# Moving the scatters of slot numbers and the first expert's weights in an attention + mixture-of-experts kernel

## The chip, the core and the metric

The kernel runs on one core of a Trainium2 chip. The core has a matrix engine (PE, with its weight loads shown apart as PEld), a vector engine (DVE), a scalar engine (ACT), a general engine (POOL), and a queue engine (SP) that mostly issues DMAs; POOL issues DMAs too, the indexed ones among them. Each engine runs its own instructions in order and waits on semaphores for the others. SBUF is the on-chip memory of 128 partitions, PSUM holds what PE writes, DRAM is outside. The metric is the time of one execution in microseconds (us): before the change the median of 3 runs is 855.22 us (852.43 to 856.94).

## The reference

Two stages. Attention with a mask by hash: 6 sign bits of each query and key (against `proj`) give a bucket, and only pairs in one bucket are scored. Then a mixture of experts, where each of the 3072 tokens goes to the one expert with the largest gate logit.

```python
q_bits = (np.einsum('bhsd,dk->bhsk', q, proj) > 0)            # the same for k; 4 batches, 8 heads, 768 tokens, width 64
mask = q_bucket[:, :, :, None] == k_bucket[:, :, None, :]
scores = np.where(mask, scale * q @ k^T, -1e9)
attn = softmax(scores) @ v                                     # tokens x 512 = x
expert_idx = argmax(x @ w_gate)                                # 8 experts
gate_w = softmax(x @ w_gate) at expert_idx
y[token] = gate_w * relu(x @ w1[e]) @ w2[e]                    # w1 512x1024, w2 1024x512, e = expert_idx
```

## The kernel before, in words

**Attention** is cut into 16 groups g (a pair of heads of one batch; 4 groups a batch) and each group into 6 *cycles* c (so c runs from 0 to 97, with a tail of two; r = c % 6 is the place in the group). In a cycle PE does, in this order: two pv steps of an older unit (L337), the gate-and-output product `tok` (L353) of one older still, 12 transposes of probabilities (L305), and two units of scores for the newest (L269 and L271: the rows of bucket bits and low parts, then the high part). DVE takes the row maximum of each unit (L276 to L278), and ahead of that, in the same cycle, scales `tok`'s product (L366) and copies one of three transposed tiles (L325). ACT takes the exponentials (L286) and copies the other two. A cycle's program is also each engine's order: nothing is reordered, the schedule is written by hand.

**The heads of the next group** are prepared on POOL while a group runs. Each of the two heads is split into a rounded part and a remainder, in 12 steps by the table `SPLITS`, two in each of the six cycles: (0,0) and (0,1) in r = 0, (0,2) and (0,3) in r = 1, then the same for head 1 in r = 2 and 3, (0,4) and (0,5) in r = 4, (1,4) and (1,5) in r = 5. The last four are a copy of 64 partitions (L179) and a subtraction on the upper 64 (L180). In r = 1 POOL also turns the hash products into bits (L232, L234); SP stores them to DRAM (`masks`, L245) and POOL reads them back into the heads' tiles in r = 3 (L249, a DMA on POOL's queue). The stores of results and the loads of the next heads stand behind L245 on SP.

**Routing.** When the tokens of half a batch are through (b, hf), the generator `route` computes their expert and their slot in that expert's list, some DVE operations at a time: `go(q, 2)` in each cycle runs the next two pieces between the transposed copies and the row maxima. Its last piece, before the change, is three indexed DMAs on POOL (L437), each of which scatters 128 slot numbers into the DRAM table `slot_token`. Each has a small memset (L436) before it. `go` stands ahead of the split steps of its cycle, so on POOL the scatters come first in that cycle. For batches 0 and 1 they fall in c = 35 and 59 (first half, r = 5) and c = 42 and 66 (second half, r = 0), for batch 2 in c = 83 (r = 5) and c = 86 (r = 2, after POOL's part of c = 85). Batch 3's follow after the last cycle.

**The first expert** (the fullest after batch 2, `pick_first` in c = 85) is started while attention still runs. Its weights come in 8 loads of 512 KB (`raw`, two buffers, L587 on SP) and are taken apart in 16 parts, `chunk_part`: a rounded copy (L597) and the remainder (L598), both on POOL for this expert. Each second part frees a buffer and issues the next load. Before the change 12 of the 16 parts run in c = 86 to 95, one or two a cycle, and four in c = 96 and 97. In c = 90, SP reads the first 256 slots (`gather_ix`, L614) and POOL gathers their rows (`gather_rows`, L622). `xt` transposes those in c = 94 to 97, and `mm1(0, 0)` is the first product of the experts.

**The experts** follow from about 506 us: for each of nine phases, products with w1 (L657) and w2 (L683, L700), while POOL, ACT and DVE take the next weights apart (L600, L601) and POOL gathers and scatters rows (L622, L711).

## Time and profile before

| what | us |
|---|---|
| median of the runs (lowest, highest) | 855.22 (852.43, 856.94) |
| profiled execution, its own time | 851.78 |
| its span, first to last instruction | 850.0 |
| PE busy in the span | 796.8 (94%) |
| DVE, ACT, POOL busy | 530.9, 439.4, 492.1 |
| mean granted clock of PE | 0.974 |

A profile row gives an instruction's start, its duration, engine, line, what it writes and reads, and in brackets how long the engine sat idle before it and what ended that. "x2" merges neighbours. A row of the view of waits gives who waited for whom, the total, how often and the longest. A row of the view of stretches gives the stretch, its length, each engine's busy time and number of instructions, then the granted share of PE's clock, the share of time in which the DMA engines were busy, and GB/s. For PE, busy time near the whole span means that what matters is where it stood idle, and where its clock was cut.

### The profile page before, as it was taken

How to read it: one execution, taken by the hardware profiler on the slowest of the kernel's cores; microseconds unless marked ns; L12 is line 12 of the kernel's file. 1: busy time of each engine (PE TensorE's matmuls, PEld its weight loads, DVE VectorE, ACT ScalarE, POOL GpSimd, SP SyncE). 2: the span in 40 equal slices, each digit the busy share in tenths (PEclk: the TensorE clock that was granted, in tenths of full speed). 3: DMA queues.
4: the chain of work that ended last, by engine and by line, in shares of the span. 5: the costliest groups of instructions: out<-in, count | busy, mean ns of one | idle time of the engine just before them, and what ended most of it. 6: DMA issues, size and time to landing. Idle time of an engine off the chain costs nothing. (4 is left out here: it accounts for less than half of the span.)

```text
span 850.0 us, 14119 instructions
## 1 busy us (share of the span) xinstructions
PE 796.8 (94%) x4814; PEld 627.7 (74%) x4814; DVE 530.9 (62%) x1234; ACT 439.4 (52%) x877; POOL 492.1 (58%) x641
## 2 busy tenths in 40 slices
PE   8999999979999969999978898999999999999992
PEld 3677767657777747777645666888999999989782
DVE  6877777858778848778956565454475644434410
ACT  4776767647676746767646461343434343434210
POOL 5876657647856747765665783564363745546401
PEclk9999999989999989999989799999999999999997
DMA  9674587467568739664737251466353635466101
GB/s 232 167 144 82 121 149 149 111 78 129 119 103 154 133 35 138 138 99 93 107 81 112 77 101 20 151 198 189 100 173 106 188 128 165 140 176 181 37 11 32
DMA packets 75804, 103.01 MB, mean 121 GB/s; under 512 B 43972, under 2 KB 48068, under 8 KB 75730
## 3 DMA queue, kind: packets, MB, share of 16 engines
q1 hardware_dynamic: 62610, 86.47, 46.0%
q0 software_dynamic: 13120, 15.61, 7.8%
q8 instruction: 39, 0.64, 0.3%
q14 instruction: 35, 0.29, 0.1%
HBM read 86.65 MB, written 16.35 MB: 121 GB/s over the span
## 5 line engine op out<-in xcount | busy, mean ns | idle before, releaser
L286 ACT ACTIVATE e<-s,m 128x768 f32<-128x768 f32 x192 | 190.4, 992 | 139.9 <-DVE m L278 134.4
L276 DVE TENSOR_REDUCE m<-s 128x1 f32<-128x768 f32 x192 | 182.9, 952 | 84.0 <-PE s L271 79.3
L337 PE MATMUL o<-pt,vt 128*64 128x384 f32 x768 | 150.3, 514 | 0.0
L305 PE MATMUL t<-ident,e 128*128 128x128 f32 x1152 | 144.4, 275 | 1.7 <-ACT pt L327 1.1
L305 PEld LDWEIGHTS t<-ident,e 128*128 128x128 f32 x1152 | 130.7, 142 | 6.8 <-issue 1.8
L657 PE MATMUL t<-xh,w 128*128 128x456 f32 (+6 forms) x672 | 127.2, 346 | 1.2 <-DVE hh L662 1.2
L657 PEld LDWEIGHTS t<-xh,w 128*128 128x128 f32 x672 | 119.1, 188 | 4.5 <-DVE hh L662 1.6
L601 POOL TENSOR_TENSOR w<-raw,w 128x512 fp32r<-128x512 f32 x56 | 72.6, 1305 | 68.5 <-ACT w L600 68.1
L327 ACT ACTIVATE pt<-t 128x512 f32<-128x512 f32 (+1 forms) x194 | 103.8, 592 | 3.1 <-PE t L305 2.4
L601 DVE TENSOR_TENSOR w<-raw,w 128x512 fp32r<-128x512 f32 x56 | 61.0, 1093 | 51.8 <-ACT w L600 43.8
L337 PEld LDWEIGHTS o<-pt,vt 128*64 128x64 f32 x768 | 47.7, 139 | 60.7 <-issue 59.7
L683 PE MATMUL t<-hh,w 128*128 128x456 f32 (+3 forms) x384 | 78.7, 358 | 0.0
L711 POOL DMA_INDIRECT out_dram<-y,ix x27 | 35.2, 1305 | 70.8 <-DVE y L709 61.9
L661 ACT ACTIVATE hh<-t 128x256 fp32r<-128x256 f32 (+7 forms) x64 | 31.3, 490 | 79.6 <-PE t L657 77.3
L683 PEld LDWEIGHTS t<-hh,w 128*128 128x128 f32 x384 | 69.9, 188 | 2.4
L271 PE MATMUL s<-qk 128*128 128x384 f32 x204 | 56.0, 357 | 16.1 <-POOL qk L180 16.1
L325 DVE COPY pt<-t 128x512 f32<-128x512 f32 (+1 forms) x97 | 66.4, 685 | 6.8 <-PE t L305 2.7
L353 PEld LDWEIGHTS t<-gm,ot 128*128 128x128 f32 x192 | 28.6, 189 | 56.7 <-issue 29.5
L662 DVE SCALAR_TENSOR_TENSOR hh<-t,hh 128x256 fp32r<-128x256 f32 (+7 forms) x64 | 35.4, 554 | 51.7 <-ACT hh L661 48.3
L269 PE MATMUL s<-qk 80*128 80x384 f32 x204 | 59.8, 373 | 8.1 <-DMA qk<-masks 4.9
L600 ACT ACTIVATE w<-raw 128x512 fp32r<-128x512 f32 x112 | 66.3, 623 | 0.0
L700 PE MATMUL s<-w,hh 128*128 128x512 f32 (+2 forms) x264 | 66.0, 405 | 0.0
(197 smaller groups left out, 1191.3 us busy)
## 6 DMA issues: line engine op xcount, KB each, us to landing
raw<-in_w_dram SPq DMA_DIRECT2D x64, 512.0 KB
xd<-in_qk_dram SPq DMA_DIRECT2D x36, 384.0 KB
xhe<-in_qk_dram SPq DMA_DIRECT2D x15, 768.0 KB
w<-in_qk_dram SPq DMA_DIRECT2D x28, 384.0 KB
vt<-in_v_dram SPq DMA_DIRECT2D x16, 384.0 KB
x_rows<-xs SPq DMA_DIRECT2D x64, 96.0 KB
masks<-bits SPq DMA_DIRECT2D x15, 192.0 KB
w<-masks POOLq DMA_DIRECT2D x15, 96.0 KB
```

The lines of the kernel that those rows point to most:

```text
L269: nc.tensor.matmul(p[:, a, :HALF], k[0:80, 2, c], k[0:80, 3, a * HALF:(a + 1) * HALF], start=True, stop=False)
L276: nc.vector.tensor_reduce(m[:, 0:1], p[:, :, :HALF], axis=AX.XY, op=OP.max)
L286: nc.scalar.activation(e, p[:, :, :HALF], AF.Exp, bias=m[:, 2:3], scale=m[:, 1:2], accum_out=SM[g, hf][:, t, s:s + 1])
L305: nc.tensor.transpose(p[:, x * 128:(x + 1) * 128], e[w][:, kt // 3, (kt % 3) * 128:(kt % 3) * 128 + 128], ident)
L325: nc.vector.tensor_copy(o, x)
L327: nc.scalar.activation(o, x, AF.Copy)
L337: nc.tensor.matmul(p[s * 64:(s + 1) * 64, :HALF], VT[g][:, kt, s, :], PT[u][:, s, kt, :], start=(kt == 0), stop=(kt == NT - 1))
L600: nc.scalar.activation(w[:, 0, a], r, AF.Copy)
L601: (nc.vector if a % 2 else nc.gpsimd).tensor_tensor(w[:, 1, a], r, w[:, 0, a], op=OP.subtract)
L657: nc.tensor.matmul(p[:, :c], w[:, a, d, fs], x[:, b, d, :c], start=(k == 0), stop=(k == 11))
L683: nc.tensor.matmul(p[:, :c], w[:, a, f % 4, ms], h[b][:, f, :c], start=(k == 0), stop=(k == 23))
L700: nc.tensor.matmul(p[:pw], HH[n][b][:, f, j * pw:(j + 1) * pw], w[:, a, f % 4], start=(k == 0), stop=(k == 23))
```

## The change

Three things move.

1. The scatters leave `route` and become `scatter(b, hf)`. It is called at the end of a cycle's program, after the split steps and the small copies of that cycle. For batches 0 and 1 the calls are in c = 37 and 61 (first half) and c = 43 and 67 (second half), for batch 2 in c = 79 and 85. All of these have r = 1 (the second cycle of a group, which is a pair of heads). Batch 2's first half is routed with four pieces a cycle, so that it is ready in c = 79. After attention, batch 3's scatters stand where they stood.
2. The 16 parts of the first expert's weights run two a cycle in c = 90 to 97. Of each two, the copy of the second goes to DVE; remainders stay on POOL. `raw_load(0, 0)` and `(0, 1)` stay in c = 85.
3. `gather_ix(0)` stays in c = 90, `gather_rows(0)` goes to c = 91.

```diff
-    scat = []
+    scat, SL = [], {}
...
         nc.sync.dma_start(xr[t0 * 128:(t0 + 3) * 128, DM:RW].rearrange("(t p) o -> p t o", p=128), f[:, 3, :, None])
-        yield
+        SL[b, hf] = slot
+
+    def scatter(b, hf):
+        slot = SL.pop((b, hf))
+        t0 = b * NT + hf * 3
         for t in range(3):
             nc.gpsimd.memset(C["spacer"], 0.0)
             st = nc.gpsimd.indirect_dma_start(
...
         if c < 4:
-            nc.gpsimd.tensor_copy(w[:, 0, a], r)
+            (nc.vector if a % 2 else nc.gpsimd).tensor_copy(w[:, 0, a], r)
             nc.gpsimd.tensor_tensor(w[:, 1, a], r, w[:, 0, a], op=OP.subtract)
...
-        for q in routes:
-            go(q, 2)
+        for q, n in routes:
+            go(q, n)
...
         if c >= 24 and c < NC:
             b, q = divmod(c - 24, 24)
+            late = b == B - 2
             if q == 4:
-                routes.append(route(b, 0))
-            if q == (7 if b == B - 2 else 11):
-                routes.append(route(b, 1))
+                routes.append((route(b, 0), 4 if late else 2))
+            if q == (7 if late else 11):
+                routes.append((route(b, 1), 2))
+            if q == (7 if late else 13):
+                scatter(b, 0)
+            if q == (13 if late else 19):
+                scatter(b, 1)
...
-        if NC - 10 <= c < NC:
-            weights(2 if c % 5 == 1 else 1)
...
         if c == NC - 6:
             gather_ix(0)
+        if c == NC - 5:
             gather_rows(0)
-        if c >= NC:
+        if c >= NC - 6:
             weights(2)
...
     go(last[0], 9)
+    scatter(B - 1, 0)
...
     go(last[1], 9)
+    scatter(B - 1, 1)
```

How the rows move on the engines. First POOL around the scatters of batch 0's first half. Before, in c = 35 (qk and xd are the heads' tile and the loaded head, slot_token the table, DMASW are the semaphores of POOL's own DMAs):

```order
L373 COPY lg<-xs 128x16 [waits DVE_49,Pool_49]
L436 MEMSET spacer 1x1
L437 DMA slot_token<-tokid_i,slot 25600x1
L436 MEMSET spacer 1x1 [waits Pool_49]
L437 DMA slot_token<-tokid_i,slot 25600x1
L436 MEMSET spacer 1x1 [waits Pool_49]
L437 DMA slot_token<-tokid_i,slot 25600x1
L179 CAST qk<-xd 64x384
L180 TENSOR_TENSOR qk<-xd,qk 64x384 [waits DMASW6_49,DMASW5_49,DMASW4_49]
```

The L180 that follows (head 1's first remainder, step (1,4)) waits for the three scatters themselves. In the changed kernel, from the third scatter of c = 37 on (w_2259 and w_2394 are the two heads' tiles of the next group):

```order
L441 DMA slot_token<-tokid_i,slot 25600x1
L173 CAST w_2394<-w_69 128x768 [waits DMAHW3_49,DMAHW4_49,DMASW1_49,PE_49]
L175 CAST w_2394<-w_69 128x768
L373 COPY lg<-xs 128x16 [waits DVE_49]
L177 TENSOR_TENSOR w_2394<-w_69,w_2394 80x384 [waits Pool_49]
L177 TENSOR_TENSOR w_2394<-w_69,w_2394 80x384
L249 DMA w_2259<-masks 16x4x384 [waits DMAHW4_49,DMASW7_49]
L249 DMA w_2394<-masks 16x4x384 [waits Pool_49]
L373 COPY lg<-xs 128x16 [waits DVE_49]
L179 CAST w_2259<-w_69 64x384
L180 TENSOR_TENSOR w_2259<-w_69,w_2259 64x384 [waits DMASW5_49,DMASW6_49,DMASW4_49,Pool_49]
```

The wait for the scatters now stands on step (0,4) of r = 4, with the splits of r = 2 and 3 and both mask reads between. The mask reads are now behind three scatters on POOL's own queue.

Second, POOL in c = 86 and 87. Before (w_5373 is the first weight chunk, w_5369 the last group's second head):

```order
L175 CAST w_5369<-xd 128x768
L373 COPY lg<-xs 128x16 [waits DVE_49]
L597 CAST w_5373<-raw 128x512 [waits DMAHW2_49,PE_49]
L598 TENSOR_TENSOR w_5373<-raw,w_5373 128x512 [waits Pool_49]
L597 CAST w_5373<-raw 128x512
L598 TENSOR_TENSOR w_5373<-raw,w_5373 128x512 [waits Pool_49]
L177 TENSOR_TENSOR w_5369<-xd,w_5369 80x384 x2
L249 DMA qk<-masks 16x4x384 [waits DMAHW7_49,DMASW6_49]
```

Now:

```order
L175 CAST w_5369<-xd 128x768
L373 COPY lg<-xs 128x16 [waits DVE_49]
L177 TENSOR_TENSOR w_5369<-xd,w_5369 80x384 [waits Pool_49]
L177 TENSOR_TENSOR w_5369<-xd,w_5369 80x384
L249 DMA qk<-masks 16x4x384 [waits DMAHW7_49]
```

Nothing that waits for a weight load stands ahead of the last group's splits and masks.

Third, DVE between c = 91 and 92 in the changed kernel (w_5597 is the first weight chunk there):

```order
L276 TENSOR_REDUCE m<-s 128x1 [waits PE_49,Activation_49]
L277 TENSOR_SCALAR m<-m 128x1 [waits DVE_49]
L278 TENSOR_SCALAR m<-m 128x1 [waits DVE_49]
L601 CAST w_5597<-raw 128x512 [waits DMAHW3_49]
L366 TENSOR_TENSOR xs<-t,r 128x144 [waits DMAHW5_49,DMAHW6_49,PE_49,Pool_49]
L325 COPY pt<-t 128x2x2x128 [waits PE_49]
```

Before, L366 follows L278 directly there. The new cast waits for a weight load's landing, and L366 and L325, which free the PSUM tiles that PE writes next, are behind it.

## The prediction

> **What bounds the kernel now.** I began with the page: PE is busy for 796.8 of 850.0 us, so a gain can only come from where PE stands still or runs at a lower clock. Next I read the view of waits. Its rows for the part that the change touches:
>
> ```profile
> POOL qk L180 <- DMA slot_token<-tokid_i,slot: 31.3, 3, 11.7
> ...
> PE s L271 <- POOL qk L180: 16.1, 3, 6.6
> ...
> PE s L269 <- DMA qk<-masks: 4.9, 1, 4.9
> ```
>
> Three times POOL's L180 waits for scatters to land, 31.3 us in all, and three times PE waits for that L180. POOL in order of time shows the first case, c = 35:
>
> ```profile
> 174.44 0.96 POOL L437 DMA_INDIRECT slot_token<-tokid_i,slot  x1 [0.22 <-issue]
> 175.41 0.51 POOL L179 CAST qk<-xd 64x384 fp32r<-64x384 f32 x1
> 185.21 0.98 POOL L180 TENSOR_TENSOR qk<-xd,qk 64x384 fp32r<-64x384 f32 x1 [9.29 <-DMA slot_token<-tokid_i,slot]
> ```
>
> From the last scatter's end (175.40) to L180 are 9.8 us; with the longest wait (11.7) it is 12.2. This L180 is head 1's first remainder, which PE needs at once in the next group. What a case costs in all is read from the view of stretches. A stretch runs from one cycle's first transpose to the next cycle's. First come two undisturbed ones (with and without hash products), then c = 36, 60 and 84, then c = 85 to 86, c = 90, 91 and 95, and a piece behind the first stall:
>
> ```profile
> 122.17:127.56 5.39, 5.39 (x40) 3.56 (x39) 3.80 (x10) 3.56 (x9) 2.13 (x3) 1.00 0.10 33
> 453.14:457.76 4.62, 4.62 (x33) 3.41 (x32) 3.73 (x11) 3.40 (x8) 1.23 (x2) 1.00 0.48 120
> 179.38:191.71 12.33, 7.99 (x40) 4.03 (x39) 4.51 (x12) 3.56 (x9) 6.28 (x9) 0.72 0.22 39
> 301.09:315.14 14.05, 7.44 (x40) 4.02 (x39) 4.50 (x12) 3.55 (x9) 5.76 (x9) 0.76 0.26 30
> 425.42:438.01 12.59, 7.46 (x40) 4.04 (x39) 4.18 (x13) 3.68 (x9) 5.78 (x9) 0.73 0.38 77
> 442.63:448.52 5.89, 4.81 (x32) 3.37 (x31) 4.74 (x17) 3.24 (x7) 4.53 (x8) 1.00 0.64 113
> 462.36:476.62 14.26, 8.06 (x32) 4.92 (x31) 3.90 (x10) 3.93 (x10) 13.49 (x20) 0.69 0.45 108
> 476.62:481.90 5.28, 5.28 (x31) 4.07 (x30) 3.50 (x9) 2.83 (x5) 3.16 (x5) 0.87 0.13 35
> 495.92:501.19 5.27, 5.04 (x34) 3.65 (x33) 4.01 (x12) 3.85 (x9) 3.49 (x5) 1.00 0.82 145
> 184.45:191.27 6.82, 5.02 (x18) 1.47 (x18) 1.33 (x3) 0.00 (x0) 5.87 (x9) 0.50 0.00 1
> ```
>
> The excess over 5.39 is 6.94 (c = 36), 8.66 (c = 60) and 7.20 us (c = 84). That is more than the 16.1 us of waits: the other 6.7 us, 2.2 a stall, are the half clock (0.50 in the last row) that follows each. PE, not POOL, sets the length of every other cycle, so these microseconds are on the path.
>
> The fourth stall is c = 90, 14.26 − 4.62 = 9.64 us, and 0.66 more in c = 91. POOL and PE in order of time show its cause:
>
> ```profile
> 456.44 0.61 POOL L597 CAST w<-raw 128x512 fp32r<-128x512 f32 x1 [8.86 <-DMA raw<-in_w_dram]
> 457.14 1.28 POOL L598 TENSOR_TENSOR w<-raw,w 128x512 fp32r<-128x512 f32 x1
> ...
> 462.80 0.56 POOL L249 DMA_DIRECT2D w<-masks  x1
> ...
> 468.76 0.98 PE L269 MATMUL s<-qk 80*128 80x384 f32 x2 [4.92 <-DMA qk<-masks]
> ...
> 472.29 1.01 PE L271 MATMUL s<-w 128*128 128x384 f32 x2 [1.27 <-POOL w L180]
> ```
>
> In c = 86 POOL waits 8.86 us for the weights' first load, in front of the last group's splits and mask reads. Those go out at 463.36, land 5.4 us later, and PE waits for them and then for head 1.
>
> **The change, part by part.** *Removed:* the four stalls, 6.94 + 8.66 + 7.20 + 9.64 + 0.66 = 33.1 us, if nothing takes their place. c = 86 keeps its excess (5.89): there DVE's `pick_first` stands in the way, and that stays.
>
> *The scatters, moved behind r = 1.* The work is the same, three L437 with their memsets: in c = 35 from 171.00 to 175.40, 4.4 us of POOL. What must now hide it is the time until PE needs the heads. A group without scatters (its second head's tile is called w too):
>
> ```profile
> 251.30 1.65 POOL L234 TENSOR_SCALAR bits<-bits,thr,mul 64x384 f32<-64x384 f32 x1
> ...
> 256.82 1.10 POOL L249 DMA_DIRECT2D w<-masks  x2
> ...
> 259.88 1.01 POOL L180 TENSOR_TENSOR w<-w,w 64x384 fp32r<-64x384 f32 x1
> ...
> 264.55 1.01 POOL L180 TENSOR_TENSOR w<-w,w 64x384 fp32r<-64x384 f32 x1
> ...
> 273.58 0.60 PE L269 MATMUL s<-w 80*128 80x384 f32 x2
> ...
> 274.72 0.52 PE L271 MATMUL s<-w 128*128 128x384 f32 x2
> ```
>
> Count from L234's end, T = 252.95. The mask reads are out by T+5.0, head 0's first remainder starts at T+6.9, head 1's ends at T+12.6. PE needs the masks at T+20.6 and head 1 at T+21.8. With the scatters between, POOL is 4.4 us later: mask reads out by T+9.4, the first L180 not before T+11.3. That L180 now carries the wait. The scatters end at T+4.6 (0.2 for the L373 between). For their landing the slow bound is the 12.2 us above. The fast one is after the last cycle, where SP's L614 waits for the very last scatter:
>
> ```profile
> 524.40 0.96 POOL L437 DMA_INDIRECT slot_token<-tokid_i,slot  x1 [0.23 <-issue]
> ...
> 531.36 0.36 SPq L614 DMA_DIRECT2D ix<-slot_token  x1
> ```
>
> That is 6.0 us. So they land at T+10.6 to T+16.8, and L180 waits 0 to 5.5 us. From that L180's start to the end of head 1's take 5.7 us in the rows above, or 4.4 without POOL's idle time, so head 1 is ready at T+17.0 to T+21.2, before T+21.8. The wait goes into POOL's slack. I take nothing for it, but the margin at the slow end is 0.6 us.
>
> What is behind the scatters on POOL's queue are the mask reads. Fast bound: the 5.4 us of c = 90. Slow bound: in the quiet group PE did not wait, so at most 273.58 − 257.92 = 15.7 us. They would be in at T+14.8 to T+25.1, against T+20.6. DMA traffic is heavy from L234 on, as the stores and loads on SP stand behind L245:
>
> ```profile
> 247.00:253.00 6.00, 6.00 (x44) 3.83 (x42) 4.36 (x14) 3.90 (x8) 3.16 (x2) 1.00 0.00 0
> 253.00:261.00 8.00, 8.00 (x55) 6.25 (x52) 5.82 (x14) 6.16 (x12) 6.59 (x12) 1.00 0.84 116
> 261.00:273.00 12.00, 12.00 (x79) 8.37 (x78) 10.43 (x28) 7.84 (x17) 6.31 (x10) 1.00 0.97 216
> ```
>
> I take the middle, T+20, just in time, and 0.6 us in all for a group that misses it. Five groups are exposed (prepared in c = 36, 42, 60, 66 and 78); in c = 85/86 POOL's order around the scatters is the old one.
>
> *The weights, moved to c = 90 to 97.* POOL splits nothing there. A pair costs POOL 0.61 + 2 × 1.28 = 3.2 us of a cycle of 4.62, so POOL keeps up, and c = 86 to 89 lose their wait with nothing put in its place. A buffer is free after the pair, and its next load must be in two cycles later: 3.2 us and the load in 9.2 us, so 6 us for a load. Two rows of stretches bound that: 131 GB/s in 4 us is one load, 89 GB/s in 12 us is two, 6 each:
>
> ```profile
> 445.70:457.70 12.00, 12.00 (x77) 8.37 (x76) 9.38 (x22) 7.63 (x15) 3.06 (x6) 1.00 0.81 89
> 470.70:474.70 4.00, 2.73 (x9) 1.18 (x10) 2.33 (x6) 1.08 (x2) 3.69 (x7) 0.50 0.40 131
> ```
>
> It fits, at the slow end without margin.
>
> *DVE's eight casts.* The nearest row is L198, the only fp32r cast of DVE:
>
> ```profile
> L198 DVE CAST qk<-xd x2: 350/355/360, 6.8 to 7.1; 128x384 fp32r<-128x384 f32 x1, 80x384 fp32r<-80x384 f32 x1
> ...
> 442.79 0.21 DVE L278 TENSOR_SCALAR m<-m 128x1 f32<-128x1 f32 x1
> ...
> 444.56 0.31 DVE L366 TENSOR_TENSOR xs<-t,r 128x144 f32<-128x144 f32 x1
> ```
>
> By columns, 0.36 × 512/384 = 0.48 us. They stand between L278 and L366, and the other two rows show what extra work there costs: in c = 85 it kept L366 back by 1.56 us, and the cycle took 5.89 − 4.62 = 1.27 more, so 0.3 us is free. A cast costs PE 0.2 (0.48 in c = 94 and 95, where `xt` already uses the slack, row 495.92). Six casts count, those of c = 96 and 97 have no scores behind them: 0 to 2.9 us (six times 0.48). I take 4 × 0.2 + 2 × 0.48 = 1.8, and 0.7 for a load that is late once: 2.5.
>
> *The rest* I cost at nothing. The gather in c = 91 finds its indices landed, and `xt` needs it three cycles later. Batch 2's routing, four pieces a cycle, is the same operations, in the 0.9 us that DVE has free in a quiet cycle (3.73 of 4.62); without that cover four pieces of 0.2 us in three cycles are 2.4 us. On SP the later weight loads wait for POOL's pairs from c = 91 on, and behind them stand only stores of results; in c = 86 to 88 nothing blocks SP any more.
>
> **Sum:** 33.1 − 0.6 − 2.5 = 30.0 us, on the profiled execution's 851.78 gives 821.8. That execution was 3.4 us under the median of the runs. Part of their spread should be these waits, so I say **823**.
>
> **Rivals.** *The tail pays.* POOL's two-input operations hold DVE up:
>
> ```profile
> 492.14 1.28 POOL L598 TENSOR_TENSOR w<-raw,w 128x512 fp32r<-128x512 f32 x1
> 492.35 1.11 DVE L346 TENSOR_SCALAR r<-sm 128x6 f32<-128x6 f32 x1
> ```
>
> A tiny operation takes 1.11 us and ends as POOL's does. If each of the six casts stands behind one remainder, it costs 0.48 + 1.28 − 0.3 = 1.46 us, 8.8 in all: 851.8 − 33.1 + 8.8 + 0.6 = 828, and 834 with each load a microsecond over its 6. For it: both engines work on the same pair. Against: POOL's first remainder should be over 2.6 us into the cycle, the cast comes at 4.9. The Trainium skill's "SBUF — State Buffer", section "Who interferes with whom", says so generally: a DVE cast in a two-port mode and a GpSimd operation exclude each other for a whole instruction, whichever starts first. By that rule the copies on POOL block DVE as well. The L346 row agrees; no row shows a DVE cast of this size.
>
> *Some groups still wait.* Masks or head 1 come 1 to 3 us late in three of the five groups, 2.2 of half clock each: 10 to 16 us more, 832 to 838. The traffic speaks for it, the margins against.
>
> *The wait only changes its place.* The scatters, now in the heavier traffic, take 16 us: head 1 at T+25, 3.2 + 2.2 = 5.4 us in each of five groups, 27: 851.8 − 33.1 + 2.5 + 27 = 848. Against it: 12.2 was the longest of three.
>
> *Slower: the mask reads queue behind the scatters* and start only as those have landed, T+16.8. With 5.4 to 15.7 us of their own they come at T+22.2 to T+32.5, 1.6 to 11.9 late; at the middle 6.8 + 2.2, five times, 45 us: 851.8 − 33.1 + 2.5 + 45 = 866. It decides from 3.9 us late (T+24.5), where five times 6.1 eats the gain of 30.6. That both use POOL's queue speaks for it; against it, a scatter is 128 numbers of four bytes, and after attention the last of six was through in 6.0 us.
>
> **How the numbers follow.** Forecast 0.62 (its own range 816 to 829), tail 0.17 (828 to 834), some groups 0.10 (832 to 838), changed place 0.06 (848), slower 0.05 (866). The range 816 to 838 leaves out the last two and some ends. Under 0.5% (4 us) a measurement of this kernel tells nothing: half of the fourth case counts as same, the rest as faster: faster 0.92, same 0.03, slower 0.05.
>
> **What would show it.** Right: no wait of PE for POOL's L180 or for masks, clock 1.00 from 20 to about 480 us, c = 36, 60, 84 at 5.4 us and c = 90 near 4.6. POOL's wait for slot_token stays, on r = 4's L180, at 0 to 5.5 us. Wrong: PE waits at a group's start for masks (fourth rival), or cycles of 6 us and more in c = 91 to 96 with L601 casts on DVE over 1 us (first).

## The result, and the profile after

The changed kernel takes **827.67 us** (median of 4 runs, 824.81 to 830.18); the kernel before took 854.33 beside it (4 runs, 852.43 to 856.94). The ratio is **0.9685, 95% interval 0.9643 to 0.9727**: 26.7 us less. The prediction said 823, range 816 to 838. Its sum, made against the profiled execution, said 821.8; the profiled execution of the changed kernel took 824.81, with a span of 822.9.

First the page of the changed kernel (busy times, and the granted clock in 40 slices of 20.6 us):

```profile
PE 787.4 (96%) x4814; PEld 624.5 (76%) x4814; DVE 535.4 (65%) x1242; ACT 440.1 (53%) x877; POOL 489.0 (59%) x633
PEclk9999999999999999999999998999999999999997
```

PE's busy time has fallen by 9.4 us, the span by 27.1. Work done at half clock counts as busy, so the 9.4 is mostly half clock that has gone: of the dips only those in slice 25 (508.6 us, behind attention) and at the end are left.

The view of waits of the changed kernel, the rows that answer to those of before (waited for, in all, times, longest):

```profile
POOL qk L180 <- DMA slot_token<-tokid_i,slot: 18.6, 4, 5.8
POOL w L180 <- DMA slot_token<-tokid_i,slot: 10.4, 2, 5.3
...
PE o L638 <- DMA xd<-x_rows,ix: 5.7, 2, 3.1
PE t L412 <- DVE oh L406: 1.5, 2, 0.9
PE t L305 <- DVE xs L366: 1.2, 4, 0.4
PE s L269 <- DMA qk<-masks: 0.8, 1, 0.8
```

POOL still waits 29.0 us in all for scatters to land (31.3 before), but in six pieces, and nobody waits for POOL's L180 any more: 16.1 and 1.3 us of PE's waits have gone. The mask wait is down from 4.9 to 0.8. New at the top is PE's wait for `xd`, the second gather, behind attention: 5.7 us, where before it was 1.2. (Line numbers have moved: the scatters' L437 is L441 now, the casts' L597 is L601, and L634 is L638.)

The view of stretches of the changed kernel, each from a cycle's first transpose to the next cycle's. In order: c = 36, 60, 78, 84, 89, 90, 91, 92, 94, 95, and a piece behind attention (length, then busy time of PE, PEld, DVE, ACT and POOL, then clock, DMA share and GB/s):

```profile
179.12:184.51 5.39, 5.39 (x40) 3.56 (x39) 4.42 (x12) 3.57 (x9) 3.48 (x6) 1.00 0.49 86
293.65:299.04 5.39, 5.39 (x40) 3.56 (x39) 4.41 (x12) 3.58 (x9) 3.49 (x6) 1.00 0.32 65
379.30:385.91 6.61, 6.00 (x47) 3.71 (x46) 5.12 (x16) 4.06 (x10) 2.16 (x3) 1.00 0.00 1
409.25:414.64 5.39, 5.39 (x40) 3.56 (x39) 4.06 (x12) 3.57 (x9) 0.00 (x0) 1.00 0.87 156
434.38:439.32 4.94, 4.82 (x33) 3.38 (x32) 3.46 (x9) 3.13 (x7) 1.54 (x3) 1.00 0.91 176
439.32:444.91 5.59, 4.83 (x32) 3.42 (x31) 3.46 (x9) 3.14 (x7) 5.26 (x9) 1.00 0.22 46
444.91:450.08 5.17, 4.82 (x32) 3.37 (x31) 5.03 (x11) 3.10 (x8) 4.93 (x7) 1.00 0.01 3
450.08:455.24 5.16, 4.83 (x33) 3.39 (x31) 4.06 (x11) 3.53 (x7) 4.77 (x5) 1.00 0.91 243
...
460.34:465.60 5.26, 5.04 (x34) 3.65 (x33) 4.92 (x13) 4.03 (x10) 3.95 (x5) 1.00 0.54 148
465.60:471.00 5.40, 5.05 (x35) 3.66 (x34) 4.17 (x12) 3.68 (x8) 3.26 (x4) 1.00 0.82 137
505.15:515.60 10.45, 4.71 (x14) 3.72 (x14) 0.96 (x3) 0.75 (x2) 3.03 (x5) 0.67 0.50 161
```

The four stalls are gone: c = 36, 60 and 84 take 5.39 us (12.33, 14.06 and 12.59 before), c = 90 takes 5.59 (14.26 before). Four places are slower than a quiet cycle of the same kind: c = 78 (1.23 more than before), c = 89 and 90 (0.3 and 1.0), c = 91 to 95 (about 0.5 each, 0.1 in the last), and the stretch behind attention, where PE works 4.7 of 10.5 us and the clock is 0.67.

I keep two numbers of each profile, to tell attention from what follows: the **lead** is how much earlier than in the kernel before (504.73 us) the first transpose of c = 97 starts, and the **rest** is the time from there to the end of the span. The changed kernel has a lead of 29.9 us and a rest of 348.1, against 345.3 before: 2.8 us of the lead are lost again behind attention.

### The profile page after: what moved, and what is told of

It is laid out like the page before. It is cut to its first block, busy times and chain, and to the rows that moved or that the text cites. A ratio compares the mean times of both kernels' runs of the same rounds, so it can differ in the third digit from the quotient of the medians.

```text
span 822.9 us, 14117 instructions
## 1 busy us (share of the span) xinstructions
PE 787.4 (96%) x4814; PEld 624.5 (76%) x4814; DVE 535.4 (65%) x1242; ACT 440.1 (53%) x877; POOL 489.0 (59%) x633
## 5 line engine op out<-in xcount | busy, mean ns | idle before, releaser
L337 PE MATMUL o<-pt,vt 128*64 128x384 f32 x768 | 145.1, 499 | 0.0
L661 PE MATMUL t<-xh,w 128*128 128x456 f32 (+6 forms) x672 | 127.2, 346 | 1.2 <-DVE hh L666 1.2
L661 PEld LDWEIGHTS t<-xh,w 128*128 128x128 f32 x672 | 119.1, 188 | 4.5 <-DVE hh L666 1.6
L325 DVE COPY pt<-t 128x512 f32<-128x512 f32 (+1 forms) x97 | 66.3, 684 | 5.5 <-PE t L305 1.3
L704 PEld LDWEIGHTS s<-w,hh 128*128 128x128 f32 (+2 forms) x264 | 47.9, 185 | 11.3
```

What stands on the lines that cost most here:

```text
L325: nc.vector.tensor_copy(o, x)
L337: nc.tensor.matmul(p[s * 64:(s + 1) * 64, :HALF], VT[g][:, kt, s, :], PT[u][:, s, kt, :], start=(kt == 0), stop=(kt == NT - 1))
L661: nc.tensor.matmul(p[:, :c], w[:, a, d, fs], x[:, b, d, :c], start=(k == 0), stop=(k == 11))
L704: nc.tensor.matmul(p[:pw], HH[n][b][:, f, j * pw:(j + 1) * pw], w[:, a, f % 4], start=(k == 0), stop=(k == 23))
```

## The experiments

Twelve runs followed, in four groups (after_again is the changed kernel itself once more); the kernels of a group ran on one chip beside the kernel before, whose median is given for each group because it differs from chip to chip by up to 7 us. All ratios are to the kernel before of the same group. Line numbers are those of the changed kernel. The lead and the rest are those of each kernel's one profiled execution; between the two profiles of the changed kernel alone they differ by 3.1 and 3.4 us.

| kernel | median us (runs) | before, median | ratio, 95% interval | lead | rest |
|---|---|---|---|---|---|
| the change | 827.67 (4) | 854.33 | 0.9685 (0.9643 to 0.9727) | 29.9 | 348.1 |
| scat_alone | 836.28 (4) | 851.38 | 0.9800 (0.9747 to 0.9854) | 20.4 | 350.6 |
| tail_alone | 847.38 (10) | 851.38 | 0.9928 (0.9899 to 0.9958) | 6.2 | 348.8 |
| casts_pool | 826.50 (4) | 851.38 | 0.9693 (0.9642 to 0.9744) | 29.9 | 349.6 |
| route_433 | 825.06 (4) | 851.38 | 0.9673 (0.9621 to 0.9724) | 29.9 | 349.5 |
| raw_late | 829.82 (4) | 858.25 | 0.9656 (0.9635 to 0.9677) | 27.1 | 351.0 |
| scat_r3 | 853.06 (10) | 858.25 | 0.9947 (0.9912 to 0.9982) | 6.6 | 352.9 |
| scat_r5 | 841.27 (5) | 858.25 | 0.9805 (0.9789 to 0.9821) | 20.1 | 348.3 |
| xt_late | 828.17 (4) | 858.25 | 0.9637 (0.9608 to 0.9666) | 25.0 | 350.2 |
| after_again | 828.94 (5) | 855.51 | 0.9688 (0.9665 to 0.9712) | 26.8 | 351.5 |
| combo | 823.50 (5) | 855.51 | 0.9626 (0.9601 to 0.9651) | 28.3 | 347.3 |
| combo2 | 824.56 (5) | 855.51 | 0.9645 (0.9619 to 0.9670) | 34.3 | 352.4 |
| combo3 | 819.96 (5) | 854.95 | 0.9599 (0.9573 to 0.9625) | 33.1 | 345.8 |

### The two halves apart: scat_alone and tail_alone

The first has the scatters and batch 2's routing as in the change, and weights, casts and gather as before; the second the other way round. The edit of the first, against the changed kernel:

```diff
-            (nc.vector if a % 2 else nc.gpsimd).tensor_copy(w[:, 0, a], r)
+            nc.gpsimd.tensor_copy(w[:, 0, a], r)
...
+        if NC - 10 <= c < NC:
+            weights(2 if c % 5 == 1 else 1)
...
             gather_ix(0)
-        if c == NC - 5:
             gather_rows(0)
-        if c >= NC - 6:
+        if c >= NC:
             weights(2)
```

> The kernel before with the scatters and batch 2's routing moved as in the change, but the weights, their casts and the first gather where they were. Theory (the two halves of the change add up): c = 36, 60 and 84 take 5.4 us instead of 12.3 to 14.1, c = 80 to 82, 41 and 65 give 1.4 us, c = 78 loses 1.2 as in the change; the stall of c = 90 (9.6 us) stays. In all 23 us less than before: 831 us, ratio 0.973. Rival (the halves need each other: POOL, 9 us in the wait for weights in c = 86, then reaches the scatters and splits of the last groups too late): c = 84 to 90 lose more than before and the time is 836 or more.

> The kernel before with the weights, DVE's casts and the first gather moved as in the change, but the scatters where they were. Theory (the halves add up, and the shortfall of 3.3 us against the prediction's sum lies in this half): the stall of c = 90 goes from 9.6 to about 1 us, the casts add 2.4 us in c = 91 to 95, and about 3 us of the lead are lost again behind attention: 4.3 us less than before, 850 us, ratio 0.995. The prediction's own sum for this half (10.3 less, 2.5 more): 846.5, ratio 0.991. The stalls of c = 36, 60, 84 stay in both.

In scat_alone c = 36, 60 and 84 take 5.39 us, as in the change. The stall of c = 90 stays, and is longer than before the change. The view of stretches for c = 90, of scat_alone:

```profile
440.16:456.25 16.09, 8.07 (x33) 4.92 (x31) 3.90 (x10) 3.94 (x10) 15.33 (x22) 0.61 0.43 114
```

That is 16.09 against 14.26. The lead is 20.4 us where 23 were expected: 1.8 are lost here, the others in c = 72 and 81. The median says 15.1 us less than the kernel before on the same chip, 8 us short of the theory's 23, and c = 90 is the place that the rival named. But only 2.6 of the 8 are missing from the lead; the rest is 5.3 longer than in the kernel before. So the scatters' move alone gives less than its three stalls (22.8 us), and c = 90 accounts for the smaller part of what is missing.

In tail_alone the three scatter stalls stay (12.8, 13.4 and 13.1 us). The rows of c = 36 and c = 90:

```profile
180.14:192.95 12.81, 8.11 (x40) 4.13 (x39) 4.51 (x12) 3.66 (x9) 6.28 (x9) 0.73 0.22 43
465.08:469.69 4.61, 4.61 (x32) 3.40 (x31) 3.45 (x9) 3.13 (x7) 2.03 (x3) 1.00 0.00 0
```

c = 90 is fully quiet: the mask reads of group 15 land 4.2 us before c = 90 begins, where in the change they land 1.3 us after (the part on group 15 below says why). c = 88 takes 6.14 us, 1.5 more than quiet; the trace names no cause for that. The ratio, 0.9928 (0.9899 to 0.9958), lies between the 0.995 of the theory and the 0.991 of the prediction's sum and settles nothing between them. The traces speak on the place of the shortfall, though: the rest is 348.8 here and **350.6 in scat_alone, whose code behind attention and whose weights are those of before**. So a loss behind attention comes without moving the weights too. By leads, 20.4 + 6.2 = 26.6 against 29.9 for both: the halves add up to within 3.3 us, about what two executions of the change differ by, so nothing can be said of what one half gains from the other.

### The price of the casts on DVE: casts_pool

```diff
-            (nc.vector if a % 2 else nc.gpsimd).tensor_copy(w[:, 0, a], r)
+            nc.gpsimd.tensor_copy(w[:, 0, a], r)
```

> The changed kernel with the eight casts back on POOL (POOL then needs 0.61 x 2 + 1.3 x 2 + 0.3 = 4.1 us of a cycle of 4.62). Theory (each cast costs what it takes on DVE between L278 and L366): c = 91 to 95 go back from 5.1 to 5.4 to 4.6 to 4.9 us, PE's waits for DVE xs L366 go, 2.4 us less than the changed kernel: 825. Rival (not the cast but POOL's two-input remainders hold DVE up, whoever does the cast): the cycles stay above 5.0 and the time is 827 or more, as POOL runs for longer in each cycle.

First the casts in the changed kernel: the group of L601 on DVE (durations in ns, smallest, median, largest), and DVE in order of time at the start of c = 93:

```profile
L601 DVE CAST w<-raw x8: 416/560/1126, 445.3 to 476.7; 128x512 fp32r<-128x512 f32 x8
```

```profile
455.54 0.75 DVE L601 CAST w<-raw 128x512 fp32r<-128x512 f32 x1
456.20 0.29 DVE L366 TENSOR_TENSOR xs<-t,r 128x144 f32<-128x144 f32 x1
```

L366 stands 0.66 us later than it would behind the maxima, and PE's next transposes wait for it. With the casts on POOL, c = 91, 92 and 93 of casts_pool:

```profile
446.86:451.47 4.61, 4.61 (x32) 3.40 (x31) 4.06 (x11) 3.42 (x8) 4.45 (x7) 1.00 0.02 4
451.47:456.07 4.60, 4.60 (x32) 3.39 (x31) 3.50 (x9) 3.14 (x7) 4.04 (x6) 1.00 0.70 198
456.07:460.67 4.60, 4.60 (x32) 3.39 (x31) 3.46 (x9) 3.13 (x7) 4.44 (x7) 1.00 0.72 122
```

They are back at 4.60, though POOL is now busy for 4.0 to 4.5 us of each. So the casts cost 0.5 us each where PE's scores stand behind them, and POOL's remainders cost nothing there by themselves: in these cycles the theory holds and the rival falls. In c = 95 the rival has a point. DVE's L641, a copy of two columns, takes 0.88 us there (0.17 in the change) and ends with a remainder of POOL's, `xt`'s L643 stands behind it, PE waits 0.7 us for that, and c = 95 takes 5.78 where the change took 5.39 and the theory said 4.9 at most. The time, 826.50, cannot be told from the change's (its lead is the same 29.9: in this execution masks came late in c = 72, which cost 1.5 us, and c = 81 cost 0.7).

### What c = 78 lost: route_433

```diff
-            go(q, n)
+            go(q, n[c % 3] if isinstance(n, tuple) else n)
...
-                routes.append((route(b, 0), 4 if late else 2))
+                routes.append((route(b, 0), (3, 3, 4) if late else 2))
```

`SL[b, hf] = slot` also moves up to where the slot is made, since the generator no longer ends in c = 79.

> The changed kernel with batch 2's first routing in portions of 4, 3, 3 and the rest instead of 4, 4, 4, so that the one-hot (L406, DVE) and the matrix products that read it (L412, PE) fall into different cycles. Theory (c = 78 is longer by 1.23 us because PE stands in its own queue for the one-hot made in the same cycle): c = 78 takes 5.4 to 5.6 us, c = 79 at most 0.3 more than now, and the time is 1 us less: 826.7. Rival (the DVE work itself delays the maxima and nothing waits for the one-hot alone): c = 78 keeps 0.6 us or more of its excess and c = 79 gains as much.

The stretches of c = 78 and 79 in route_433:

```profile
378.81:384.42 5.61, 5.61 (x41) 3.56 (x40) 4.78 (x14) 3.96 (x9) 2.18 (x3) 1.00 0.01 1
384.41:389.32 4.91, 4.91 (x39) 3.60 (x38) 4.10 (x13) 3.58 (x8) 4.15 (x5) 1.00 0.08 26
```

c = 78 falls from 6.61 to 5.61, c = 79 rises from 4.60 to 4.91: 0.7 us, near the theory's 1. By its time the kernel cannot be told from the change (ratios 0.9673 and 0.9685). Four pieces in one cycle put the one-hot (L406) and the products that read it (L412) into the same cycle, and PE, in its own order, stood 0.6 us before the first of those products and then started the next scores late.

### Where the landing must not fall: scat_r3 and scat_r5

These move the scatters of the five exposed groups to other places in the group: behind r = 3's mask reads, or behind r = 5's splits.

```diff
-            if q == (7 if late else 13):
+            if q == (9 if late else 15):
                 scatter(b, 0)
-            if q == (13 if late else 19):
+            if q == (13 if late else 21):
                 scatter(b, 1)
```

> The changed kernel with the scatters of the five exposed groups two cycles later, behind r = 3's splits and mask reads, so that the mask reads stand in front of the scatters. Theory (what costs is the landing: the next operation on the upper half of the partitions, L180 of r = 4, waits for it and both heads come behind it): scatters end near T+10, land 3.8 to 11.9 us later, L180's wait is as long as before or longer, and head 1 is ready at T+19 to T+27 against T+21.8: PE waits for L180 in two to four of the five groups, 1 to 5 us each and half clock behind it, 8 to 20 us more than the changed kernel: 836 to 848. Masks have 4 us more of slack. Rival (the queue is what matters: whatever stands behind the scatters is late): masks gain 4 us, nothing else changes, 827 or less.

POOL in order of time in group 6 of scat_r3:

```profile
192.10 1.10 POOL L249 DMA_DIRECT2D w<-masks  x2
...
197.53 0.96 POOL L441 DMA_INDIRECT slot_token<-tokid_i,slot  x1 [0.23 <-issue]
210.94 0.99 POOL L180 TENSOR_TENSOR w<-w,w 64x384 fp32r<-64x384 f32 x1 [11.92 <-DMA slot_token<-tokid_i,slot]
```

PE in the same stretch, and the cycle (c = 42):

```profile
211.98 0.62 PE L271 MATMUL s<-w 128*128 128x384 f32 x2 [2.24 <-POOL w L180]
...
215.38 1.01 PE L271 MATMUL s<-w 128*128 128x384 f32 x2 [2.44 <-POOL w L180]
```

```profile
207.92:221.08 13.16, 8.49 (x41) 4.19 (x39) 3.89 (x10) 3.77 (x9) 9.39 (x14) 0.74 0.25 60
```

Two cycles later in the same group, and the stall is back: 13.16 us for c = 42, 11.28 for c = 66, 9.92 for c = 72. L180's waits grow to 52.1 us in all (29.0 in the change), and the kernel is 22 us slower than by the change's ratio, almost back at the kernel before; those three cycles make up 18 of it. The masks, in front of the scatters, came in by T+10.1 to T+17.6 (T, as in the prediction, is the end of L234) against T+14.6 to T+17.0: their place on the queue was not what mattered. The theory holds, at more than its upper figure.

> The changed kernel with the scatters behind r = 5's splits (batch 2's first routing then goes two pieces a cycle as before the change; the scatters of c = 85 stay). Theory (any place will do whose next operation on the upper half has more than the landing time of slack): the wait moves to L234 of r = 1, 0 to 5 us; c = 36, 60 and 84 stay at 5.4, c = 78 falls from 6.61 to 5.4, c = 80 to 82 take 0.3 to 0.6 us more each as the two routings overlap; masks have as much slack as now or up to 3 us less. Same time as the changed kernel within 2 us: 825.5 to 829. Rival (behind r = 5 they meet the loads of the next group and land later, over 12 us): L234 and with it the masks come late in two or more groups, 3 to 6 us each: 834 or more.

scat_r5's edit puts `scatter(b, 0)` at q = 11 and `scatter(b, 1)` at 17 (13 for the late batch), with two pieces a cycle throughout. c = 36, 60 and 84 stay at 5.4, L234 waits for the scatters only 1.1 us in all, c = 78 is back at 5.4: so far the theory. But c = 38 takes 7.57 us and c = 61 and 62 6.0 each, 1.4 more than quiet, and the kernel is 1.2% slower than the change. (Its profile is of the fastest of its five executions, 6.4 us under their median, so not all of the loss is in the trace.) For c = 38 the reason, which lies in c = 37, is neither the landing nor the masks. DVE and then POOL of scat_r5:

```profile
186.70 3.23 DVE L346 TENSOR_SCALAR r<-sm 128x6 f32<-128x6 f32 x1
```

```profile
186.24 0.85 POOL L173 CAST w<-w 128x768 fp32r<-128x768 f32 x1
187.01 0.83 POOL L175 CAST w<-w 128x768 fp32r<-128x768 f32 x1
187.78 0.20 POOL L373 COPY lg<-xs 128x16 f32<-128x16 f32 x1
187.95 1.95 POOL L177 TENSOR_TENSOR w<-w,w 80x384 fp32r<-80x384 f32 x2
```

An operation on six elements, 0.16 us elsewhere, took 3.23 and ended with POOL's chain at 189.9. The scatters and a POOL wait just ahead of them had pushed POOL's splits into one piece without a gap, and it fell on L346; PE then waited 2.7 us for L366, which stands behind L346. c = 62 is the same (L346 takes 1.91 us). c = 61 is not: there PE and ACT stood for 1.1 and 1.7 us with no releaser that the trace names, and I leave it open. Neither my theory nor its rival had this.

The Trainium skill, "SBUF — State Buffer", section "Who interferes with whom", says that a DVE `tensor_scalar` can run in a two-port mode, and that it and a GpSimd instruction then exclude each other: whoever issues first has the ports for the whole instruction. The trace agrees in that DVE's instruction ended when POOL's were through; but it stood beside five POOL instructions in a row, not one. That the ports held it is inferred from the times.

### Group 15's masks: raw_late

```diff
         if c == NC - 11:
             pick_first()
+        if c == NC - 8:
             raw_load(0, 0)
             raw_load(0, 1)
```

> The changed kernel with the first two weight loads issued three cycles later (c = 88 instead of 85). Theory (the two loads of 512 KB, issued at 425 us, stand on the DMA engines in front of group 15's mask reads, issued at 430.3, whose packets start only at 437.1): the mask packets start by 434, the masks are in 4 us or more before PE needs them instead of 0.9, PE's wait for them (0.76) goes and c = 90 takes 4.6 to 4.8 us instead of 5.59; the time is 1 to 3 us less (the half clock that a late mask brings in some runs goes too). Rival (the mask reads are late because they stand behind the three scatters of c = 85, whatever else is under way): first packets at 436 or later, c = 90 stays at 5.2 us or more, same time.

The mask packets start 4.3 us after their issue instead of 6.8, but the last one is in 10.8 us after it (10.3 in the change). c = 90 is quiet (4.59), yet only because c = 89 has become worse:

```profile
435.80:444.12 8.32, 6.36 (x32) 4.34 (x31) 3.80 (x10) 4.29 (x9) 4.77 (x8) 0.79 0.88 165
```

In it DVE's L366 waits 2.3 us, PE waits for it, and half clock follows. No gain, and the theory is not borne out: the reads take about as long with the loads 1.1 us behind them as with the loads 5.3 us ahead of them.

### The transposes behind attention: xt_late

```diff
-    mm2(0, 1, lambda: xts(1, (0, 1)))
-    xts(1, (2, 3))
+    mm2(0, 1)
+    xts(1, (0, 1, 2, 3))
```

> The changed kernel with the transposes of the second gather's rows (L638 on xd) behind the whole second output tile of the first phase instead of in its middle, 12 products of 0.4 us = 4.8 us later. Theory (behind attention the chain from the last scatter over the index load and the gather to these transposes ends last, PE stands 3.6 to 5.7 us for xd, and half clock follows): the wait falls to under 1 us, the half clock near 509 us goes in most runs, and 1 us comes back since the transposes are now exposed: 3 us less than the changed kernel, 824.5. Rival (the gather's rows come late because PE's and DVE's own steps ahead of the last scatter are late, and PE meets the next wait anyway): xd's wait goes, but the first expert's second phase starts no earlier, 827.

In the changed kernel, PE in order of time behind attention:

```profile
499.61 5.54 PE L704 MATMUL s<-w,qk 128*128 128x512 f32 x23
508.25 0.33 PE L638 MATMUL o<-ident,xd 128*128 128x128 f32 x1 [3.09 <-DMA xd<-x_rows,ix]
511.22 0.47 PE L638 MATMUL o<-ident,xd 128*128 128x128 f32 x1 [2.65 <-DMA xd<-x_rows,ix]
```

In xt_late no wait for xd is left in its profile; 0.8 us of waiting for DVE stands in its place. That is not shown to be the edit's doing: PE had lost 1.8 us in c = 97 and 2.6 us at L661 on the way, so it came later, and combo, which has the same edit, still waits 3.8 us for xd. Its ratio of 0.9637 is the lowest of the single edits, 0.5% under the change's on other chips (the interval's end touches that of after_again, so this alone does not prove a gain). Its profile shows something else besides. In c = 97, DVE and then PE:

```profile
484.43 0.43 DVE L601 CAST w<-raw 128x512 fp32r<-128x512 f32 x1 [1.82 <-DMA raw<-in_w_dram]
484.77 0.42 DVE L643 TENSOR_TENSOR xhe<-t,xhe 128x256 fp32r<-128x256 f32 x1
```

```profile
485.24 0.50 PE L661 MATMUL s<-xhe,w 128*128 128x256 f32 x2 [1.84 <-DVE xhe L643]
```

A weight load is late; the cast that waits for it stands on DVE in front of `xt`'s L643, and PE waits for that. With the cast on POOL that wait would not stand in front of L643; no run shows that with a late load.

### Putting them together: after_again, combo, combo2, combo3

combo is casts_pool, route_433 and xt_late in one. combo2 also has the first weight loads in the program of c = 90, takes the weights apart from c = 92 on, and does the last four parts behind mm1(0, 0). combo3 has the loads in c = 89 and takes two parts a cycle in c = 91 to 95 and three in c = 96 and 97. combo3 against combo:

```diff
         if c == NC - 11:
             pick_first()
+        if c == NC - 7:
             raw_load(0, 0)
             raw_load(0, 1)
...
-        if c >= NC - 6:
-            weights(2)
+        if c >= NC - 5:
+            weights(2 if c < NC else 3)
```

> The changed kernel once more, beside the next two on one chip. Ratio 0.967 to 0.969 as before. The lead at the start of c = 97 is 28 to 30 us; behind attention the wait for xd's rows (0 to 6 us) and half clock of 3.4 or 6.8 us vary from one execution to the next, so its time is 0 to 5 us over the lead.

> The changed kernel with the casts on POOL, batch 2's first routing in portions of 4, 3, 3, and the transposes of xd behind the second output tile, all three at once. Theory (the three costs are separate): c = 78 and 79 give 0.7 us, c = 91 to 95 give 2.4 us and a late weight load no longer holds up DVE, the wait for xd gives 1 to 3 us: 4 to 6 us less than the changed kernel on the same chip, ratio to it 0.993 to 0.995. Rival (the gather of the first phase's second part sets the end there whatever comes before it: a shorter attention only lengthens the wait for xd): 1 to 2 us less.

> As the kernel with all three, and the first weights are loaded from c = 90 on (instead of 85), split from c = 92 on, and the last four parts are split behind mm1(0, 0). Theory (c = 88 to 90 lose 0.4 to 3.7 us since stores of x_rows, group 15's mask reads and 1 MB of weights share the DMA engines from 425 to 440 us): c = 88 to 90 take 4.6 to 4.8 us each, and the time is 1 to 3 us less than that of the kernel with all three. Rival (weights then come too late: PE waits at the start of mm1 for w, or the last scatters stand behind the four parts on POOL and xd comes later): a wait of PE for w or a longer one for xd of 2 us or more, and the time is the same or up to 5 us more.

> As the kernel with all three (casts on POOL, routing 4, 3, 3, xd's transposes later), and the first weights are loaded from c = 89 on, split two parts a cycle in c = 91 to 95 and three in c = 96 and 97, so that none is left for POOL behind attention. Theory (what the kernel with the last four parts behind mm1(0, 0) won in c = 88 to 90 it gave back because POOL's splits stood in front of the last scatters and kept DVE's small operations waiting): c = 88 to 90 take 14 to 15 us in all, the last scatter starts 18 to 19.5 us after c = 97 begins against 24.5 there, and the ratio to the kernel before is 0.957 to 0.961, that is 820 to 822. Rival (the weights' loads, six of them now in four cycles, cannot keep up, POOL ends as late as there, and stores of x_rows come behind them on SP): the last scatter starts over 22 us after c = 97 begins, ratio 0.963 or more.

The changed kernel repeats: 0.9688. Its second profile has c = 89 at 7.77 us (4.94 in the first), so a lead of 26.8; in its rest of 351.5 PE loses 1.6 us in c = 97, and half clock of 3.41 us near 768 us comes on top. So much, 6.5 us of span, differs between two executions of one program.

**combo** is 5.4 us faster than the change beside it (823.50 against 828.94, intervals of the ratios apart), as its theory said.

**combo2** has c = 88 to 90 quiet: 4.62, 4.62 and 4.60 us, 13.84 in all. That does not show the loads to be the cause. SP runs ahead of the cycles in these traces: the two loads of raw_late (program of c = 88), combo3 (c = 89) and combo2 (c = 90) leave SP at the same place, 1.7 us after c = 88 began (at 431.18, 428.57 and 429.32). SP in order of time of the three, in this order:

```profile
432.92 1.31 SPq L591 DMA_DIRECT2D raw<-in_w_dram  x2
...
430.28 1.06 SPq L591 DMA_DIRECT2D raw<-in_w_dram  x2
...
431.04 1.05 SPq L591 DMA_DIRECT2D raw<-in_w_dram  x2
```

Yet c = 88 to 90 take 17.5, 14.75 and 13.84 us in them. With the loads ahead of the mask reads the three cycles take 13.8 to 18.9 (casts_pool 13.8, the change 15.2, after_again 17.4, combo 18.9). It is one execution each, and they differ more from one execution to the next than by the place of the loads.

Of combo2's lead of 34.3 us, 6.0 more than combo's, almost nothing arrives: the rest is 352.4, 5.1 longer than combo's, and the median is not lower. POOL and then DVE of combo2, behind attention:

```profile
484.38 0.61 POOL L601 CAST w<-raw 128x512 fp32r<-128x512 f32 x1 [3.31 <-DMA raw<-in_w_dram]
485.07 1.28 POOL L602 TENSOR_TENSOR w<-raw,w 128x512 fp32r<-128x512 f32 x1
...
488.44 1.04 POOL L441 DMA_INDIRECT slot_token<-tokid_i,slot  x1 [0.16 <-DVE rl L399]
```

```profile
487.16 1.12 DVE L399 TENSOR_TENSOR rl<-rl,rf 128x24 f32<-128x24 f32 x1
```

The last weights stand on POOL in front of the last scatters, and they hold up the routing on DVE as well (L399, 24 elements, 1.12 us beside L602). The last scatter starts 24.5 us after c = 97 began; in the change it is 20.1, in combo 19.7. The rival that named this was right.

**combo3** leaves POOL nothing there. Its last scatter starts 21.6 us after c = 97 began, short of the 18 to 19.5 expected (PE waits twice for the one-hot, 2.7 us in all, before it), so the theory's mechanism came only in part, though the time came out as it said: **819.96 us, ratio 0.9599 (0.9573 to 0.9625)**, faster than the kernel before and than the change (0.9685 and 0.9688; the intervals do not meet).

## Why the prediction was right, and where it was not

**The stalls and their size: right.** They were to go, 33.1 us in all. c = 36, 60 and 84 gave 6.94, 8.67 and 7.20, c = 90 gave 8.67 of 9.64. Nothing waits for L180 of POOL any more, and the clock is 1.00 from 20 to 508 us, so the half clock went with the stalls.

**The scatters behind r = 1: right in its steps.** POOL in order of time in c = 37 to 40 of the changed kernel:

```profile
186.54 1.66 POOL L234 TENSOR_SCALAR bits<-bits,thr,mul 64x384 f32<-64x384 f32 x1
...
195.95 1.14 POOL L249 DMA_DIRECT2D w<-masks  x2
...
202.82 1.00 POOL L180 TENSOR_TENSOR w<-w,w 64x384 fp32r<-64x384 f32 x1 [5.09 <-DMA slot_token<-tokid_i,slot]
...
206.26 1.00 POOL L180 TENSOR_TENSOR w<-w,w 64x384 fp32r<-64x384 f32 x1
```

T is 188.20, the mask reads are out by T+8.9 (predicted T+9.4), L180 waits 5.1 us (0 to 5.5; the longest is 5.8), head 1 is ready at T+19.1 (T+17.0 to 21.2). Over the five groups it is T+17.0 to T+19.7, and the masks were in at T+14.6 to T+17.0, at the early end of the span of T+14.8 to T+25.1 that I had left open. The mask reads did not wait for the scatters to land, as the fourth rival had it: in this group their first packet starts at 199.2, and the last scatter lands at 202.7. The 0.6 us allowed for a late group did not come in the profile, but did in another execution: 1.5 us in c = 72 of casts_pool. scat_r3 showed how narrow the place is: 6.2 us later on POOL, and 22 us are lost.

**Group 15: overlooked.** I left it out as "the old order", but its masks come 0.76 us late in c = 90 (one of my own signs of being wrong), and DVE waits 0.4 us for an x_rows store in c = 89, which costs 0.3. Two things had changed there. First, POOL comes to the group late: the stall of c = 84 had covered the load of the heads that POOL takes apart there. POOL's view of waits in the changed kernel has a row that the kernel before has not:

```profile
POOL qk L173 <- DMA xd<-in_qk_dram: 7.2, 1, 7.2
```

L234, from which the mask reads follow, ends 3.3 us after c = 86 begins; before the change it ended 0.9 us ahead of c = 86. Second, the mask reads no longer stand behind weight parts on POOL, so they go out 5.3 us after the first weight load instead of 16.5, and are in 10.3 us later instead of 4.9. tail_alone tells the two apart: there the loads are as close (3.8 us ahead) and the reads take the same 10.3 us, but the stall of c = 84 is still there, L234 ends 0.9 us ahead of c = 86, and the masks are in 5.5 us before PE needs them (4.0 without the 1.5 that c = 88 loses there). So the late heads, not the loads alone, use up the slack. In other executions c = 88 to 90 lose up to 5 us; how much of that is the loads' doing stays open. That the reads would come up to the loads could have been read from the order of before and after.

**The casts: the right place, too small a price.** The step was "0.3 us is free. A cast costs PE 0.2", 1.8 in all. In a run of such cycles nothing was free: a cast costs its full 0.5, and c = 91 to 96 lost 2.5 (0.55 + 0.55 + 0.50 + 0.44 + 0.12 + 0.31). The 0.3 came from c = 85, a single late cycle; that its neighbours' slack absorbed it is my guess. The first rival (a cast behind a remainder, 1.46 each) did not come: at most 0.79 in c = 91 to 95. The 0.7 for a late load did not cost PE in this profile, and cost 1.84 in that of xt_late. That the term as a whole (1.8 + 0.7) equals the 2.5 measured is luck.

**Batch 2's routing: costed at nothing, cost 1.2 us, gave 1.4.** Counting DVE's free time was the wrong test; the wait was PE's, for L406 in the same cycle (route_433). On the other side I had not counted that c = 80 to 82, 41 and 65 become quiet, 1.4 us, as the scatters and the two routings no longer fall together. The two errors cancel, by luck.

**Behind attention: the term that was missing.** Up to c = 97 the sum came out almost exactly: 30.0 predicted, 29.6 measured (29.9 less 0.3 by which this execution was ahead from the start). Part of that is luck: c = 89 and 90 lost 1.3 and the casts 0.7 that the sum did not have, and the 0.6 for a late group and the 0.7 for a late load were not spent. The 2.8 us lost after it make up the miss of 3.0. The wait for xd went from 1.2 to 5.7 us, and half clock of 6.83 us followed. The last scatter is 29.5 us earlier, so the chain from it over the index load and the gather to L638 kept its lead up to there; the second gather's rows then landed 1.5 us later after their issue than before, and PE, which no longer lost 2.6 us to DVE on the way, came sooner. scat_alone lost even more with the code of before behind attention, and the kernel before has one profile only, of an execution 2.5 us under its median. And all the other kernels' rests, 345.8 to 352.9, are longer than that one's 345.3. So this may be mostly how that one execution happened to run, and I cannot say how much the change adds.

**The last step, from the sum to 823, went the right way but not far enough.** The profiled execution was 3.4 us under the median, and I added 1.2 of that, arguing that part of the runs' spread was in the waits removed. It was not: the spread was 4.5 us and is 5.4 us now, and the median moved by 26.7 us; the two profiles of the changed kernel differ in c = 89 and behind attention. The sum taken off the median of 855.22 gives 825.2.

## What to carry to other kernels

A transfer's landing is paid by the next instruction that waits on it, so move its issue to where that instruction has more slack than the longest landing: two cycles' difference was worth 22 us here. When a stall goes, ask what it had been hiding and what comes forward with it: here the load of the last group's heads (7.2 us of POOL's time) and mask reads that came up to the weight loads. A shorter attention can be given back at the chain behind it: of combo2's 6 us of lead over combo, its profile keeps 1 and its median none. And read from the queue when a transfer really goes out; its place in the program does not tell. On DVE and POOL look at which small operation stands in front of what PE needs next, not at the share of free time.

## What was not expected of the hardware

- A DVE operation on six elements took 3.23 us beside five POOL instructions in a row (scat_r5; 0.16 elsewhere), one on 24 elements 1.12 us beside one of POOL's (combo2).
- Scatters of 128 numbers each land 3.8 to 11.9 us after their issue in the changed kernel (median 8.9, of the 16 of 24 whose landing the trace gives), and POOL waited up to 11.9 us for them in scat_r3. All have the same size, so it is not the size that sets it; that it is the traffic was not tested.
- Half clock comes, but for the end of the program, in pieces of 3.41 us or two, three or four of them, and the length of PE's wait does not tell how many: 6.83 us after 5.7 us of waits for xd in the change, 3.41 after 3.8 in scat_alone, none after 3.2 in tail_alone, but 3.41 after a single wait of 1.96 us in c = 89 of raw_late. The Trainium skill, "TensorE: Matmul & The Clock Gate", section "What's actually happening", gives a free-running window of 3413 ns for this; the pieces agree with it.
